# Three weight conversions behind the first layer norm, and other PSUM banks for two token products, in a fused scan, Fourier and MLP kernel

## The chip, the cores and the metric

The kernel runs on one core of one Trainium2 chip, as one launch. The metric is device microseconds from the first to the last moment of the execution, median over runs. The engines are named as the profile names them: PE (TensorE; PEld is its weight load), DVE (VectorE), ACT (ScalarE), POOL (GpSimd) and SP (the engine that issues all DMAs of this kernel).

## What is computed

All arrays are fp32: 4 batches, 8 heads, 768 tokens, head size 48, so 384 channels.

```python
# 1 a linear recurrence per head, complex decay a clipped to modulus 0.999
S = a[t] * S + outer(k[t], v[t]);  y[t] = q[t] @ Re(S)
# 2 Fourier mixing, then a layer norm and a channel MLP (384 -> 1536 -> 384)
u = x + Re(fft2(x));  un = layer_norm(u)
x = u + relu(un @ w_ch1) @ w_ch2
# 3 a token MLP (768 -> 256 -> 768), then a second channel MLP
u = x + (relu(x.T @ w_tok1) @ w_tok2).T
out = u + relu(u @ w_ch1b) @ w_ch2b
```

## The kernel before

Each batch goes through a **chain** and then through **dense** work. The chain is `stage1` (the scan over 48 steps and the attention-like sums per chunk of 96 tokens) and `stage2` (folds and mirrors of the transposed tokens, the real DFT as matmuls, the joins of its halves into six token tiles `u[0]` to `u[5]`, the layer norm into `un`). `stage2` handles its six tiles in three pairs (tile `i` and tile `i + 3`): a matmul result is copied out by ACT (L1188), POOL forms a difference and a sum of it (L1189, L1190), PE transposes the tokens (L1199), DVE joins both (L1204), and then come the statistics (L1211, L1212), a few tiny passes on ACT and DVE (L1221 to L1226), and one normalising pass for each tile, on DVE (L1233) or ACT (L1231). `LAST[0]` is the last normalising pass traced so far. `transposed` then turns `un` by PE and splits it in two fp32r halves, `th` (ACT, L1017) and `tl` (DVE, L1018).

Dense work is `dense1` (first channel MLP by `mlp`, then the token products `tok1` and `tok2`) and `mlp2` (second channel MLP). `mlp` runs in four quarters; each multiplies three weight blocks (L1034, with ReLU on ACT at L1038 and the low half on DVE at L1047) and adds the second product into `u` (L1056, L1059). Batch b's dense work fills PE while the chain of batch b + 1 runs; the buffer `qkt` exists once, so a scan follows the layer norm of the batch before. At the end the dense works of batches 2 and 3 are interleaved by `mixed`, and their `tok1` and `tok2` are called `late`.

**Conversions.** The weights arrive as 64-bit floats and are split into two fp32r halves on the chip. `convert` does one weight half of 128 x 384: a read into a tile of pool `T` (L206), ACT passes (L214 into a PSUM tile, L219), a DVE shift (L227), a POOL addition (L229), a DVE pass for the sign (L233), an ACT copy that rounds (L239), a POOL subtraction (L240) and a write to DRAM (`wscr`, L244). It is a generator: `tick` moves all generators in `active` on by one step, `feed` runs what is left to its end. Eight weights (p below 4) are kept in SBUF; twelve more (`back`) go through `convert` without a kept tile and are read again later (L320); the other 36 are converted during the first dense work by `lead`, in the form of L222 and L225, with the PSUM bank `c`, and the reads of the first few of these are ordered behind work of the MLP (`hold`).

Of the twelve, two are through before `stage2` of batch 0; **eight** are started at the sixth chunk and advanced once at the seventh (ACT passes); they are the eight in `active` when `stage2` reaches its five ticks (L1140, L1141). In order they hold the weights (13,0), (13,1), (14,0), (14,1), (15,0), (15,1), (4,1) and (6,1). The remaining two, (8,1) and (10,1), are done by `feed(56)` at L1321, after the first `transposed`.

**Order.** The program is traced in the order of the code; a planner then places every instruction on its engine's queue by priority and by a simulated time, and gives a tile its buffer when one of its pool is free. Priorities go by stream: for ACT, DVE and POOL the first chain and the dense work come first, then the conversions, then the other chains. `rests[0]` and `rests[1]` order a conversion's DVE passes and its POOL addition behind a given instruction in that plan (`rest`, `after`); this is an order of the planner, not a semaphore. Each engine then executes its queue in order, SP too.

**Buffers that matter.** Pool `T` has eight tiles: those of the conversions, and `th`, `tl`, `xh`, `xl`. PSUM has eight banks: two `s`, three `l`, two `p`, one `c`. A request for `s` takes turns over `s`, `s`, `c` (over `s` alone, or `s` and `p`, during the chain of batch 1). `p` holds the scans' state and the PSUM tile of the twelve conversions; `l` the MLPs' products. In the late calls `tok1` takes its two banks, and `tok2` and `transposed` theirs, from `s`.

Of the kernel before, what the change touches and what calls it, by code (L numbers as in the profile page):

```python
# [54 lines left out]
def attn_fft_mixer_kernel(ctx: ExitStack, tc: tile.TileContext, aL, xL, vL, wL, qN, kN, vN, arN, aiN,  # L55
# [37 lines left out]
    def alloc(tag, shape, dt=F32, name=None):  # L93
        n = 1
        for x in shape[1:]:
            n *= x
        t = pool.tile([128, SIZE[tag]], dt, tag=tag, bufs=BUFS[tag], name=name or tag)
        return shaped(t[0:shape[0], 0:n], shape)
# [4 lines left out]
    def palloc(tag, shape):  # L103
        n = 1
        for s in shape[1:]:
            n *= s
        if tag == "s":
            turn3[0] += 1
            tag = ("ssc", "s", "sp")[lent[0]]
            tag = tag[turn3[0] % len(tag)]  # L110
        t = psum.tile([128, 512], F32, tag=tag, bufs=PSB[tag], name=tag)
        v = t[0:shape[0], 0:n]
        if len(shape) == 3:
            v = v.rearrange("p (a b) -> p a b", b=shape[2])
        return v

    def r32(ap):
        return ap.bitcast(F32)
# [46 lines left out]
    LAST = [None]  # L165

    def marked(x):
        if stream[0] != CHAIN:
            mark[0] = x

    def after(x, y):
        tc.add_manual_dep(x.ins, y.ins.name, HOLD, reason="order of the streams")
# [6 lines left out]
    rests = [None, None]  # L179
# [72 lines left out]
    active, begun = [], []  # L252

    def begin():
        p, j = convs.pop(0)
        return convert(p, j, ws.place if (p, j) in early else None, far=True)

    def feed(n):

        keep, stream[0] = stream[0], BACK  # L260
        for _ in range(n):
            if convs:
                for _ in begin():
                    pass
        stream[0] = keep

    def tick(n, loads=False):

        keep, stream[0] = stream[0], BACK
        active[:] = [g for g in active if next(g, "end") != "end"]  # L270
        for _ in range(n):
            g = begin()
            next(g)
            if not loads:
                next(g)
            active.append(g)
        stream[0] = keep
# [790 lines left out]
    def stage2(b, space):  # L1068
# [50 lines left out]
        def dft(kt):  # L1119
            for ty in range(4):  # L1120
                n0, n = 128 * kt, ZK[ty][kt]
                ps = palloc("s", [128, 2, 97])
                for r in range(2):
                    for dt in range(2):
                        te.matmul(out=ps[0:n, r, :], lhsT=fd[:, ty, r, dt, n0:n0 + n], rhs=dcos[0:112, ty % 2, dt, r, :],
                                  start=(dt == 0), stop=(dt == 1))
                se.copy(out=Z[0:n, 2 * ty + kt, :].rearrange("p (i r) -> p r i", r=2), in_=ps[0:n])
# [7 lines left out]
        if b == 0:  # L1135
            for o, v in kept:
                after(sp.dma_start(out=o, in_=v), x)
            marked(x)
            rests[0], rests[1] = x, None
            for _ in range(5):  # L1140
                tick(0)  # L1141
            rests[0] = None
        dft(0)

# [94 lines left out]
    def tok1(b, u):  # L1239
        xh = [alloc("T", [128, 3, 384], F32R, name="xh") for _ in range(2)]  # L1240
        xl = [alloc("T", [128, 3, 384], F32R, name="xl") for _ in range(2)]
        xh, xl = ([x[i // 3][:, i % 3, :] for i in range(6)] for x in (xh, xl))
        for i in range(6):
            se.copy(out=xh[i], in_=u[i])  # L1244
            (ve if b in XL[0] and i in XL[1] else ge).tensor_tensor(out=xl[i], in0=u[i], in1=r32(xh[i]), op=ALU.subtract)  # L1245
        if EN:
            ws.ensure(b, 12, 0, 3)
        late = b in (B - 2, B - 1)
        if late:
            Rh, Rl = (alloc("tmp", [128, 2, 384], F32R, name="R") for _ in range(2))  # L1250
        else:
            R = alloc("h", [128, 4, 384], F32R, name="R")
            Rh, Rl = R[:, 0:2], R[:, 2:4]
        pss = [palloc("s" if late else "l", [128, 384]) for _ in range(2)]
        for part in (range(KS), range(KS, 6)):
            for m2, low in ((0, 0), (1, 0), (0, 1), (1, 1)) if part[-1] < 5 else ((0, 0), (0, 1), (1, 0), (1, 1)):
                for kt in part:
                    wh, wl = ws.block(b, 12 + m2, kt)
                    for w, x in (((wh, xl),) if low else ((wh, xh), (wl, xh))):
                        te.matmul(out=pss[m2], lhsT=w, rhs=x[kt], start=(kt == 0 and not low and w is wh),  # L1260
                                  stop=(kt == 5 and low == 1))
        if EN:
            ws.ensure(b, 14, 0, EN)
        for m2 in range(2):
            ps = pss[m2]
            se.activation(out=Rh[:, m2, :], in_=ps, func=ACTF.Relu)
            ve.scalar_tensor_tensor(out=Rl[:, m2, :], in0=ps, scalar=0.0, in1=r32(Rh[:, m2, :]),
                                    op0=ALU.max, op1=ALU.subtract)
        return Rh, Rl
# [13 lines left out]
    def dense1(b, u, th, tl):  # L1283
        go(mlp(u, b, 0, th, tl, None))
        R = tok1(b, u)
        g = tok2(b, u, *R)
        go(g, 2)
        return transposed(u, None, "l", g)
# [9 lines left out]
    def mixed(g, b, u):  # L1298

        go(g, 1)  # L1300
        R = tok1(b, u)
        go(g, 1)
        go(tok2(b, u, *R))
        go(g, 10)
        t = transposed(u, None, "s")
        go(g)
        return t


    def on(s, f, *args):  # L1310
        stream[0] = s
        return f(*args)

    def chain(b):
        return stage2(b, stage1(b))
# [2 lines left out]
    sp.dma_start(out=fk, in_=cFk)  # L1318
    u, norm = on(FIRST, chain, 0)
    t1 = on(FIRST, transposed, u, norm, "s")  # L1320
    feed(56)  # L1321
    for b in range(B - 2):
        lent[0] = int(not b)
# [21 lines left out]
    with tc.If(fv != 0):  # L1345
        with tc.For_i(0, B, 1) as b:
            fallback(b)
            u, norm = stage2(B, alloc("qk", [128, 12288], name="ws"))
            t = transposed(u, norm, "s")
            dense2(B, u, *dense1(B, u, *t), row=b)  # L1350
# [111 lines left out]
```

## Time and profile before

| | us |
|---|---|
| median of 3 runs | 1027.31 |
| lowest and highest of them | 1024.51, 1028.1 |
| the profiled execution | 1025.11 |
| its span, first to last instruction | 1023.2 |
| its mean granted TensorE clock | 0.991 of full |

The profile is of one execution. Its times are microseconds from the start of the span, unless marked ns. Matmuls are pipelined: a row of many has overlapping ends, so a busy PE is not PE at its peak. In a timeline, a row may stand for several like instructions (x2), and the bracket at its end gives the idle time of the engine before it and what ended it. "issue to landing" of a DMA is from the queue's instruction to the arrival of the last byte.

### The profile page before, as it was taken

To read this page: it belongs to the slowest core of one execution; us is meant where nothing else is said; L and a number is where in the kernel's file an instruction comes from. 1 tells how busy PE (TensorE), PEld (TensorE's weight loads), DVE (VectorE), ACT (ScalarE), POOL (GpSimd) and SP (SyncE) were. 2 spreads that over 40 slices of the span, in tenths; PEclk is the share of its full clock that TensorE was granted. 3 is DMA by queue.
4 is the path that set the end of the run, shared out by engine and by line. 5 is a ranking of instruction groups with operands and counts; after the bars stand their busy time and mean duration, and the time that the engine had idled before them with its cause. 6 is when DMAs were issued, how large, how long until landed. Compare 5 with 4: busy or idle time off the path is not lost.

```text
span 1023.2 us, 21015 instructions
## 1 busy us (share of the span) xinstructions
PE 951.0 (93%) x7312; PEld 902.0 (88%) x7312; DVE 716.9 (70%) x1965; ACT 526.4 (51%) x1489; POOL 452.8 (44%) x655
## 2 busy tenths in 40 slices
PE   1479989999899999999999999999999999999997
PEld 0338869999898899999998999999989999999997
DVE  7988978889897778999668889855664333433332
ACT  7864568887995166887216667821342122211111
POOL 7744677765785673677147335614630002000000
PEclk9999999999999999999999999999999999999999
DMA  6625865886689435665734467553325345435422
GB/s 234 175 67 140 290 269 165 283 268 210 212 258 272 146 95 187 193 179 174 206 110 140 129 193 247 157 149 102 108 78 166 131 131 171 139 108 176 136 91 80
DMA packets 98337, 173.09 MB, mean 169 GB/s; under 512 B 10928, under 2 KB 57904, under 8 KB 97712
## 3 DMA queue, kind: packets, MB, share of 16 engines
q1 hardware_dynamic: 98224, 171.67, 53.8%
q8 instruction: 60, 0.98, 0.4%
q14 instruction: 53, 0.43, 0.1%
HBM read 132.31 MB, written 39.32 MB: 168 GB/s over the span
## 4 chain that ended last, share of the span: by engine, by line
PE 66%; DVE 6%; ACT 3%; DMA 2%; POOL 2%; issue 2%; SPq 0%; POOLq 0%; ACTq 0%; DVEq 0%
PE l L1056 25%; PE l L1034 23%; DMA cvt<-wL 2%; PE s L845 2%; PE s L721 2%; PE l L1260 1%; PE l L1278 1%; PE s L1260 1%; PE s L1278 1%; PE s L1152 1%; DVE qkt L1099 1%; PE s L900 1%; PE s L860 1%; PE c L721 1%; PE c L845 1%
## 5 line engine op out<-in xcount | busy, mean ns | idle before, releaser
L1056 PE MATMUL l<-w,h 128*128 128x384 f32 x1728 | 324.0, 339 | 1.5 <-DVE h L1047 1.0
L1034 PE MATMUL l<-th,w 128*128 128x384 f32 x1152 | 313.3, 341 | 2.8 <-DVE h L1047 2.5
L1056 PEld LDWEIGHTS l<-w,h 128*128 128x128 f32 x1728 | 298.2, 188 | 3.5 <-DVE h L1047 2.0
L1034 PEld LDWEIGHTS l<-th,w 128*128 128x128 f32 x1152 | 209.1, 188 | 5.8 <-DVE h L1047 3.9
L1038 ACT ACTIVATE h<-l 128x384 fp32r<-128x384 f32 x192 | 94.0, 490 | 215.9 <-PE l L1034 215.3
L1034 PE MATMUL l<-tl,w 128*128 128x384 f32 x576 | 194.6, 338 | 0.0
L1059 DVE TENSOR_TENSOR u<-u,l 128x384 f32<-128x384 f32 x192 | 105.5, 549 | 74.4 <-PE l L1056 73.4
L1047 DVE SCALAR_TENSOR_TENSOR h<-l,h 128x384 fp32r<-128x384 f32 x160 | 88.3, 552 | 88.9 <-ACT h L1038 88.8
L1034 PEld LDWEIGHTS l<-tl,w 128*128 128x128 f32 x576 | 108.4, 188 | 0.1
L229 POOL TENSOR_TENSOR cvt<-cvt 128x384 int32<-128x384 int32 x48 | 50.4, 1051 | 27.4 <-DVE cvt L225 16.5
L1245 POOL TENSOR_TENSOR xl<-u,xh 128x384 fp32r<-128x384 f32 x18 | 18.0, 1014 | 93.2 <-ACT xh L1244 93.0
L240 POOL TENSOR_TENSOR w<-cvt,w 128x384 fp32r<-128x384 f32 x44 | 45.0, 1027 | 13.1 <-ACT w L239 13.0
L1045 POOL TENSOR_TENSOR h<-full,h 128x384 fp32r<-128x384 f32 x32 | 32.5, 1016 | 34.3 <-ACT full L1044 32.8
L529 PE MATMUL s<-misc,y 128*112 128x128 f32 x64 | 14.5, 369 | 35.4 <-DVE y L511 27.9
L694 DVE TENSOR_TENSOR p<-p,A 128x144 f32<-128x144 f32 x144 | 44.7, 310 | 2.8 <-ACT A L671 1.0
L529 PEld LDWEIGHTS s<-misc,y 128*112 128x112 f32 x64 | 9.3, 177 | 41.6 <-POOL ss L496 20.3
L881 POOL TENSOR_TENSOR yc<-Aa,gm 48x384 f32<-48x384 f32 x18 | 20.6, 1147 | 53.3 <-DVE Aa L871 53.0
L670 POOL TENSOR_TENSOR A<-raw,tm 128x144 f32<-128x144 f32 (+1 forms) x51 | 25.9, 508 | 39.4 <-DVE yt L695 29.6
L696 DVE TENSOR_TENSOR p<-p,yt 128x96 f32<-128x96 f32 x144 | 37.7, 262 | 2.8
L651 POOL TENSOR_TENSOR tm<-tm 128x144 f32<-128x144 f32 (+1 forms) x51 | 25.3, 496 | 32.3 <-ACT tm L650 27.8
L695 DVE TENSOR_TENSOR yt<-p,A 128x96 f32<-128x96 f32 x144 | 36.2, 251 | 2.4 <-ACT A L674 0.5
L721 PE MATMUL s<-misc,y 128*112 128x128 f32 x222 | 35.5, 273 | 1.2 <-DVE y L708 0.8
(320 smaller groups left out, 2045.2 us busy)
## 6 DMA issues: line engine op xcount, KB each, us to landing
w<-wscr SPq DMA_DIRECT2D x180, 384.0 KB, 3.5
cvt<-wL SPq DMA_DIRECT2D x48, 384.0 KB, 4.8
wscr<-w SPq DMA_DIRECT2D x44, 384.0 KB, 4.1
Kn<-kn SPq DMA_DIRECT2D x56, 192.0 KB, 3.7
kn<-y SPq DMA_DIRECT2D x96, 96.0 KB, 2.7
raw<-aL SPq DMA_DIRECT2D x48, 144.0 KB, 3.8
xx<-xL SPq DMA_DIRECT2D x48, 144.0 KB, 3.6
V<-vL SPq DMA_DIRECT2D x32, 144.0 KB, 3.0
```

The costliest lines, as they stand in the source:

```text
L229: x = ge.tensor_tensor(out=a, in0=a, in1=lo, op=ALU.add)
L240: ge.tensor_tensor(out=parts[:, 1, :], in0=a.bitcast(F32), in1=r32(parts[:, 0, :]), op=ALU.subtract)
L694: ve.tensor_tensor(out=cur, in0=prev, in1=A[:, j, 0:3, :], op=ALU.mult)
L695: ve.tensor_tensor(out=y, in0=prev[:, 1::-1, :], in1=A[:, j, 3:5, :], op=ALU.mult)
L696: ve.tensor_tensor(out=cur[:, 0:2, :], in0=cur[:, 0:2, :], in1=y, op=ALU.add)
L721: te.transpose(ps[:, j, :], y[:, j, 0:112], ident)
L1034: te.matmul(out=ps, lhsT=w1[:, wi, kt * 128:kt * 128 + 128], rhs=x[g][:, kt, :], start=(n == 0), stop=(n == 8))
L1038: x = se.activation(out=hi, in_=ps, func=ACTF.Relu)
L1045: ge.tensor_tensor(out=lo, in0=full, in1=r32(hi), op=ALU.subtract)
L1047: ve.scalar_tensor_tensor(out=lo, in0=ps, scalar=0.0, in1=r32(hi), op0=ALU.max, op1=ALU.subtract)
L1056: te.matmul(out=ps, lhsT=hs[m][:, hi, tt * 128:tt * 128 + 128], rhs=w2[:, wi, :], start=(n == 0), stop=(n == 8))
L1059: ve.tensor_tensor(out=u[tt], in0=u[tt], in1=ps, op=ALU.add)
```

## The change

In `stage2` of batch 0 the five ticks run over the first five of the eight conversions alone; the last three are set aside in `begun` and put back into `active` afterwards. In the main program, after the first layer norm and the first `transposed`, and ahead of `feed(56)`, five more ticks finish those three, with their DVE passes and POOL additions ordered behind `LAST[0]`, the last pass of that layer norm. Apart from that, `tok1` of batches 2 and 3 takes its two PSUM tiles from `p` and not from `s`.

```diff
--- before.py
+++ after.py
@@ -1137,8 +1137,10 @@
                 after(sp.dma_start(out=o, in_=v), x)
             marked(x)
             rests[0], rests[1] = x, None
+            active[:], begun[:] = active[:5], active[5:]
             for _ in range(5):
                 tick(0)
+            active[:], begun[:] = begun[:], []
             rests[0] = None
         dft(0)
 
@@ -1251,7 +1253,7 @@
         else:
             R = alloc("h", [128, 4, 384], F32R, name="R")
             Rh, Rl = R[:, 0:2], R[:, 2:4]
-        pss = [palloc("s" if late else "l", [128, 384]) for _ in range(2)]
+        pss = [palloc("p" if late else "l", [128, 384]) for _ in range(2)]
         for part in (range(KS), range(KS, 6)):
             for m2, low in ((0, 0), (1, 0), (0, 1), (1, 1)) if part[-1] < 5 else ((0, 0), (0, 1), (1, 0), (1, 1)):
                 for kt in part:
@@ -1318,6 +1320,10 @@
     sp.dma_start(out=fk, in_=cFk)
     u, norm = on(FIRST, chain, 0)
     t1 = on(FIRST, transposed, u, norm, "s")
+    rests[:] = [LAST[0]] * 2
+    for _ in range(5):
+        tick(0)
+    rests[:] = [None] * 2
     feed(56)
     for b in range(B - 2):
         lent[0] = int(not b)
```

## Rows read from the trace of the kernel before

**Rows 1.** The page: busy time of the engines; the chain that ended last, by line.
```profile
PE 951.0 (93%) x7312; PEld 902.0 (88%) x7312; DVE 716.9 (70%) x1965; ACT 526.4 (51%) x1489; POOL 452.8 (44%) x655
...
PE l L1056 25%; PE l L1034 23%; DMA cvt<-wL 2%; PE s L845 2%; PE s L721 2%; PE l L1260 1%; PE l L1278 1%; PE s L1260 1%; PE s L1278 1%; PE s L1152 1%; DVE qkt L1099 1%; PE s L900 1%; PE s L860 1%; PE c L721 1%; PE c L845 1%
```

**Rows 2.** Stages: length; busy us of PE, PEld, DVE, ACT, POOL; clock; DMA.
```profile
152.50:170.00 17.50, 17.50 (x93) 16.57 (x93) 13.08 (x31) 15.39 (x45) 11.30 (x18) 0.91 0.46 155
...
200.00:335.00 135.00, 127.50 (x955) 120.87 (x954) 115.58 (x322) 106.73 (x302) 91.67 (x128) 1.00 0.78 247
```

**Rows 3.** Groups by line, 125 to 152.5 us: count, busy us, mean ns, idle before.
```profile
L229 POOL TENSOR_TENSOR cvt<-cvt 128x384 int32<-128x384 int32 x8 | 8.1, 1019 | 7.3 <-DVE cvt L227 7.3
L240 POOL TENSOR_TENSOR cvt<-cvt 128x384 fp32r<-128x384 f32 x8 | 8.0, 1005 | 2.3 <-ACT cvt L239 2.3
...
L233 DVE SCALAR_TENSOR_TENSOR cvt<-p,cvt 128x384 int32<-128x384 int32 x8 | 4.4, 551 | 2.3 <-POOL cvt L229 2.1
L227 DVE TENSOR_SCALAR cvt<-p 128x384 int32<-128x384 int32 x8 | 4.3, 552 | 1.5 <-ACT p L214 1.5
...
L239 ACT CAST cvt<-cvt 128x384 fp32r<-128x384 f32 x8 | 4.0, 501 | 1.1 <-DVE cvt L233 1.1
```

**Rows 4.** Timeline of DVE: start, us, line, op, out<-in, count, idle before.
```profile
137.11 0.61 DVE L1204 TENSOR_TENSOR u<-c,qkt 128x192 f32<-128x192 f32 x2
...
145.71 0.55 DVE L233 SCALAR_TENSOR_TENSOR cvt<-p,cvt 128x384 int32<-128x384 int32 x1
146.17 0.61 DVE L1204 TENSOR_TENSOR u<-s,qkt 128x192 f32<-128x192 f32 x2
```

**Rows 5.** Line L1233: count, ns min/median/max, first and last start.
```profile
L1233 DVE TENSOR_SCALAR qkt<-u,mv,rs x3: 451/478/2264, 143.4 to 151.2; 128x384 f32<-128x384 f32 x3
```

**Rows 6.** Timeline of POOL.
```profile
141.59 1.00 POOL L240 TENSOR_TENSOR cvt<-cvt 128x384 fp32r<-128x384 f32 x1
...
143.53 0.53 POOL L1189 TENSOR_TENSOR qkt<-qkt 128x193 f32<-128x193 f32 x1
...
172.84 1.08 POOL L240 TENSOR_TENSOR w<-cvt,w 128x384 fp32r<-128x384 f32 x1
```

**Rows 7.** Timeline of ACT.
```profile
140.89 0.48 ACT L1188 COPY qkt<-s 128x386 f32<-128x386 f32 x1
...
151.76 0.72 ACT L1231 ACTIVATE qkt<-u,rs 128x384 f32<-128x384 f32 x1
...
164.53 0.20 ACT L684 COPY p<-A 64x48 f32<-64x48 f32 x1
```

**Rows 8.** Timeline of PE, at four places.
```profile
141.42 0.73 PE L1199 MATMUL s<-misc,xT 112*128 112x112 f32 x4 [0.57 <-ACT qkt L1188]
...
155.15 1.34 PE L1034 MATMUL l<-th,w 128*128 128x384 f32 x3
...
178.16 0.51 PE L1034 MATMUL l<-th,w 128*128 128x384 f32 x2
...
397.52 0.33 PE L1034 MATMUL l<-th,w 128*128 128x384 f32 x1
...
762.98 0.55 PE L1012 MATMUL c<-misc,qkt 128*128 128x128 f32 x3 [0.84 <-ACT qkt L1231]
```

**Rows 9.** Timeline of DVE at the second layer norm.
```profile
395.77 0.56 DVE L1018 TENSOR_TENSOR tl<-p,th 128x384 fp32r<-128x384 f32 x1 [0.30 <-ACT th L1017]
```

**Rows 10.** Timeline of SP's queue of DMA issues.
```profile
148.55 0.88 SPq L206 DMA_DIRECT2D cvt<-wL  x2
...
163.87 2.62 SPq L206 DMA_DIRECT2D cvt<-wL  x4
```

**Rows 11.** DMA issues: count, KB each, median us from issue to landing.
```profile
cvt<-wL SPq DMA_DIRECT2D x48, 384.0 KB, 4.8
...
wscr<-cvt SPq DMA_DIRECT2D x12, 384.0 KB, 3.7
```

**Rows 12.** Line L657, scan of batches 1 to 3: ns min/median/max.
```profile
L657 DVE SCALAR_TENSOR_TENSOR tm<-tm x51: 202/301/1160, 160.3 to 657.5; 128x144 f32<-128x144 f32 x48, 128x48 f32<-128x48 f32 x3
```

## The prediction

> **What bounds the kernel now.** I read the page first: TensorE (PE) is busy in 93% of the span, VectorE (DVE) in 70%, and 48% of the chain that ended last is the two matmul lines of the channel MLPs, L1034 and L1056 [rows 1]. The reader is to see there that from the first MLP to the end the kernel is one long queue of matmuls. So the time is: the start of that queue, its work, and its idle. The queue starts at 155.15 us [rows 8], after the first batch's scan, attention, Fourier stage and layer norm, which nothing overlaps. An edit before 155.15 can move the start; an edit after it pays only where PE sits idle.
>
> Next come the stages. From 200 to 335 us PE is busy for 127.5 of 135 us, but DVE also for 115.6, ScalarE (ACT) for 106.7 and GpSimd (POOL) for 91.7 [rows 2]: the scan of batch 1 and the conversions of 36 further weights run beside the first MLPs there. Just after the start, from 152.5 to 170 us, DVE has 13.1 busy of 17.5, ACT 15.4, POOL 11.3 [rows 2]. So there the room is 4.4, 2.1 and 6.2 us.
>
> Last come the instructions of the first layer norm, engine by engine [rows 4 to 7]. Eight conversions run through it. Each costs two DVE passes of 0.55 us, two POOL passes of 1.02 and 1.01, and an ACT pass of 0.50 [rows 3].
>
> **Part one, the layer norm.** The change takes the DVE and POOL passes of the last three of the eight out of it, and puts them behind its last pass, ACT's L1231 at 151.76 [rows 7]. The first five stay where they are. What goes is 6 x 0.55 = 3.3 us of DVE, 3 x 2.03 = 6.1 us of POOL, 3 x 0.50 us of ACT's L239 and, since only two PSUM banks feed the eight, also the last one's L214 on ACT (it needs the bank that the sixth frees; priced like L239, an estimate): 2.0 us. What decides is when the joins of the third pair of token tiles (L1204) start on DVE, now 146.17 [rows 4]. Three things must come first.
> - DVE itself. The first pair's joins end at 137.11 + 0.61 = 137.72, so 8.45 us lie between. In them are five passes of the moved conversions, 0.46 apart by the starts 145.71 and 146.17 [rows 4], together 2.3; and one normalising pass, L1233, of 2264 ns where the median is 478 [rows 5], 1.8 too long. Without them the joins could start at 146.17 - 4.1 = 142.1.
> - POOL's L1189. Its input, ACT's L1188, ends at 140.89 + 0.48 = 141.37 [rows 7]; it starts at 143.53, behind a subtraction at 141.59 and one more addition [rows 6], both of moved conversions. Without them it ends near 141.9.
> - PE's transposes L1199 end at 141.42 + 0.73 = 142.15 [rows 8]. They wait for L1188, which does not move.
>
> The three meet near 142.2, **4.0 us earlier**. From there to L1231 the same work follows, so the last pass comes at 147.8 and the first MLP at 151.2. Bounds: 2.2 if only POOL's wait goes (143.53 - 141.37); 5.6 if the lower clock goes too, since 0.91 of TensorE's clock was granted from 152.5 to 170 [rows 2], so part of it ran at 1.2 of 2.4 GHz, and 9% of 17.5 us is 1.6. I take 4.0; warm-up matmuls behind the last transposes stay as they are.
>
> **What part one pays back.** The moved work needs 3.3, 2.0 and 6.1 us on DVE, ACT and POOL where there is room for 4.4, 2.1 and 6.2: it just fits. If that cover were gone it would cost the next scan what ACT lacks, and ACT is the tightest: scan 1 cannot begin before its coefficients and its first product (L684, 164.53 [rows 7]). I let 2.0 us of ACT push it: scan 1 gains 2.0, not 4.0 (bounds 0 and 4.0). It matters where the two meet again, at the second layer norm. There the last split (L1018) ends at 395.77 + 0.56 = 396.33 [rows 9] and PE turns to the second batch's MLP at 397.52 [rows 8]: slack 1.2. So PE keeps 2.0 + 1.2 = **3.2** of its 4.0 us. The next stages repeat this with the next batch; I assume they pass 3.2 on.
>
> **The queues that the moved steps pass.** On SP the three writes (L244) go later. Behind them stand the reads (L206) of the two conversions that feed issues, then the next reads of scan data. One of those two reads now needs a buffer that a moved conversion frees only after the layer norm; its DMA chain is in the second rival. On DVE the held passes carry an order of the planner and no wait, so nothing stands behind them there longer than 0.55 us each. The transposes' four tiles of the same pool find their room among the first five conversions' buffers.
>
> **Part two, the token products.** It moves the first token product of batches 2 and 3 from the banks `s` to `p`, which the scans no longer use. Nothing is added or removed. Around it PE is idle 0.84 us before 762.98, where the last layer norm's transposes and this product both want `s` and `c` banks [rows 8]. With its own banks the product can fill such a hole. At most 0.84 is to be had; at worst the turns of `s` and `c`, which now fall on other tiles, lose as much. I take a gain of **0.4**.
>
> **Sum.** 3.2 + 0.4 = 3.6 us. The profiled execution took 1025.1 us, so it would take 1021.5; the median of the runs is 1027.3, 2.2 above it, and I put the forecast on the median: **1023.7**. With the bounds of these terms the gain is 0 + 1.2 - 0.8 = 0.4 at the low end and 5.6 + 0.8 = 6.4 at the high one, so 1020.9 to 1026.9. About 0.5% (5.1 us) is what a measurement of this kernel can tell from no change.
>
> **Rivals.**
> - *All of it arrives.* PE keeps the 4.0, the lower clock goes (1.6) and the idle 0.8 too: 6.4 us, **1020.9**. For it: PE idles little after 200 us, and batch 0 has matmuls left until 397.5. Against it: scan 1 must start as early as the MLP, beside more work. 0.25.
> - *The weights come late (slower).* The place is SP's queue. The last read of feed was issued with its neighbour in the pair at 148.55; 4.8 us to landing [rows 11] make it about 153.8, and SP reached the reads of the 36 weights at 163.87 [rows 10], 10.1 us on, just behind feed's writes. After the change this read waits for the sixth conversion: DVE, POOL, DVE, ACT, POOL from 147.8 make some 152, its write lands 3.7 later [rows 11], the read 4.8 after that, 160.5; with the same 10.1 SP gets to the weights at 170.6, 6.7 us late. The first of them is subtracted at 172.84 and ready at 173.9 [rows 6], and PE wants it at 178.3 [rows 8], 174.3 after the change. One stall only: 2.3 us slower than now, 1029.6. If the conversions pace the MLP from there, all 6.7 remain: **1034.0**. What decides is whether the planner lets the reads of the 36 overtake feed's last write on SP. For it: reads of weights are 2% of the chain [rows 1]. Against: the first weight now has 178.3 - 173.9 = 4.4 us of reserve. 0.13 for the whole stream.
> - *The moved passes lengthen scan 1.* L1233 took 2264 ns beside POOL passes and 451 at best [rows 5]; scan 1's L657 takes 301 ns in the median and up to 1160 [rows 12]. If half of the six POOL passes stretch such a pass by 0.86, DVE pays 2.6 + 3.3 against 4.0: 1.9 slower, **1029.2**. 0.10. The Trainium skill (GPSIMD Engine Reference, Specifications) says that POOL shares its SBUF interfaces with VectorE, so that both contend when VectorE runs in a two-port mode or reads two SBUF inputs, as L657 does; by that rule the move takes contention out of the layer norm and puts it into the scan, and both rows agree with it.
> - *It does not do what it says.* The planner orders all engines anew, the joins start by something else, and the gain ends below 1 us: **1027**. 0.10.
>
> **How the numbers follow.** The forecast has 0.42. Faster by over 0.5% (below 1022.2): the first rival and a ninth of the forecast's own range, 0.30. Slower by over 0.5% (above 1032.4): the late weights, 0.13. Within: 0.57. The range 1019.5 to 1031.0 leaves out the slow rival and the low end of the fast one.
>
> **What would show it.** Right: L1204's third group near 142, no L1233 over 0.6 us, the first L1034 near 151, L1018 of the second layer norm 2 us earlier, L1260 writing `p`. Wrong: a first L1034 after 153; a PE wait of over 2 us near 174 for a weight; idle of over 1 us before the second batch's MLP; SP standing at L244 beyond 165.

## The result, and the profile after

The changed kernel takes **1030.84 us** (median of 9 runs, 1028.70 to 1034.47) against 1025.61 for the kernel before on the same chip (9 runs, 1023.29 to 1028.20): ratio **1.0058**, 95% interval 1.0044 to 1.0072: 5.2 us slower by the medians, 5.9 by the ratio. The forecast was 1023.7, with 13% on slower by over 0.5%. All ratios below are to runs of the kernel before on the same chip, which took 1023.3 to 1025.6 us in the median; 0.001 is 1 us. In the changed kernel the lines above 1139 keep their numbers, those of the layer norm and the token products are two higher (L1204 is L1206).

The page of the changed kernel, part 1, against [rows 1]:

```profile
span 1030.6 us, 20995 instructions
PE 955.8 (93%) x7312; PEld 905.4 (88%) x7312; DVE 719.4 (70%) x1965; ACT 526.4 (51%) x1489; POOL 451.3 (44%) x655
```

The span is 7.4 us longer. TensorE's idle (span less busy) is 74.8 us for 72.2, so 2.6 of that is idle; the other 4.8 is busy time of the same 7312 matmuls. More busy time for the same work can come from the clock, although the mean granted clock, 0.990 for 0.991, makes only about 1 us of it over the whole span (an estimate: 1% of 1030.6 less 0.9% of 1023.2); where the rest comes from is not shown. So the first look goes to the clock in the stages of the layer norm (columns as in [rows 2]: length; busy us of PE, PEld, DVE, ACT, POOL; granted clock; DMA), the changed kernel first and one stage of the kernel before behind it:

```profile
125.00:132.50 7.50, 5.93 (x49) 5.62 (x47) 5.22 (x13) 5.33 (x14) 4.68 (x5) 0.99 1.00 363
132.50:139.50 7.00, 7.00 (x28) 6.91 (x28) 4.06 (x11) 3.27 (x8) 6.06 (x8) 0.53 0.94 378
139.50:146.00 6.50, 6.48 (x42) 5.09 (x41) 4.02 (x15) 2.52 (x10) 2.10 (x4) 1.00 0.44 149
```
```profile
132.50:139.50 7.00, 7.00 (x50) 6.74 (x48) 5.24 (x14) 3.97 (x9) 7.00 (x9) 1.00 0.90 363
```

POOL needs 12.85 us in these 21 us, for 17.50 before, as intended. But TensorE, fully busy from 132.5 to 139.5, was granted 0.53 of its clock: nearly all of that stretch ran at the lower of its two levels (1.2 of 2.4 GHz). The timeline of PE there, and of the ACT copy-outs (L1190, L1188 before) that follow from it:

```profile
131.51 1.36 PE L1125 MATMUL c<-dcos,qkt 112*128 112x97 f32 x8 [1.57 <-ACT qkt L1127]
132.67 2.83 PE L1154 MATMUL s<-qkt 128*128 128x193 f32 x8
...
136.79 3.94 PE L1154 MATMUL s<-qkt 128*128 128x193 f32 x16
```
```profile
140.77 0.48 ACT L1190 COPY qkt<-s 128x386 f32<-128x386 f32 x1 [3.04 <-PE s L1154]
143.86 0.48 ACT L1190 COPY qkt<-s 128x386 f32<-128x386 f32 x1 [1.95 <-PE s L1154]
...
150.37 0.71 ACT L1233 ACTIVATE qkt<-u,rs 128x384 f32<-128x384 f32 x1
```

In the kernel before, the two groups of 8 and 16 matmuls took 1.50 and 2.81 us:

```profile
132.68 1.50 PE L1152 MATMUL s<-qkt 128*128 128x193 f32 x8
...
134.95 2.81 PE L1152 MATMUL s<-qkt 128*128 128x193 f32 x16
```

The copy-out that stood at 140.89 [rows 7] comes at 143.86, the last normalising pass at 150.37 for 151.76 [rows 7], and the first MLP follows at 153.59 for 155.15 [rows 8]. The layer norm gained 1.4 us and not 4.0. The half clock was not new, though; it had changed its place. The kernel before had it at the layer norm's end, the changed kernel there had none (before first):

```profile
146.00:156.00 10.00, 7.26 (x25) 4.36 (x23) 7.74 (x26) 7.24 (x20) 3.23 (x5) 0.66 0.54 181
```
```profile
146.00:156.00 10.00, 8.38 (x38) 5.27 (x37) 9.03 (x27) 8.06 (x26) 4.55 (x7) 1.00 0.10 30
```

That alone would still be a gain. The loss arises later. In scan 1, at its twelfth step, ACT and DVE:

```profile
202.46 0.32 ACT L658 ACTIVATE tm<-tm 128x144 f32<-128x144 f32 x1 [0.77 <-DVE tm L657]
205.18 0.51 ACT L214 ACTIVATE c<-cvt 128x384 f32<-128x384 f32 x1 [2.40 <-DMA cvt<-wL]
205.63 0.53 ACT L219 ACTIVATE cvt<-cvt 128x384 int32<-128x384 uint32 x1
206.06 0.53 ACT L222 ACTIVATE cvt<-cvt 128x384 fp32r<-128x384 int8 x1
...
207.31 0.33 ACT L671 COPY A<-A 128x144 f32<-128x144 f32 x1
```
```profile
206.62 0.56 DVE L225 SCALAR_TENSOR_TENSOR cvt<-c,cvt 128x384 int32<-128x384 int32 x1 [2.65 <-ACT cvt L222]
207.67 0.32 DVE L694 TENSOR_TENSOR p<-p,A 128x144 f32<-128x144 f32 x1 [0.49 <-ACT A L671]
```

Read it from below. The scan's step (L694) waits for ACT's L671; L671 stands in ACT's queue behind the passes of a conversion (L214 to L222); L214 waits 2.40 us for that conversion's read. L671's own input, from POOL's L670, was there by 204.3 at the latest. ACT executes its queue in order, so the scan stands behind a transfer that it has nothing to do with. In the kernel before there is the same wait for the same kind of read, but the scan's pass had gone ahead of it:

```profile
199.91 0.32 ACT L671 COPY A<-A 128x144 f32<-128x144 f32 x1
...
204.00 0.51 ACT L214 ACTIVATE c<-cvt 128x384 f32<-128x384 f32 x1 [2.21 <-DMA cvt<-wL]
```

From there on the chains are late. The table gives the starts of steps 12 and 14 of scan 1 (step 14 shows how much of the lateness stays) and of the last normalising pass of each batch, in us, from the timelines of DVE and ACT; three kernels of the experiments stand beside. Each column is one profiled execution.

| | before | changed | hold undone, order of the changed kernel kept | changed, one place repaired | hold alone, order of before |
|---|---|---|---|---|---|
| batch 0, last pass | 151.8 | 150.4 | 152.4 | 149.6 | 147.6 |
| scan 1, step 12 | 200.3 | 207.7 | 208.8 | 202.8 | 198.6 |
| scan 1, step 14 | 206.1 | 210.8 | 212.0 | 208.1 | 204.0 |
| batch 1, last pass | 390.8 | 397.5 | 402.3 | 391.7 | 387.0 |
| batch 2, last pass | 583.4 | 594.7 | 600.2 | 586.4 | 579.6 |
| batch 3, last pass | 762.2 | 773.9 | 779.5 | 765.6 | 758.4 |

TensorE itself also loses time further on, in the chain of batch 2. In the changed kernel it waits there 2.95 us, its longest wait behind the first MLP's start, for a read of `Kn` (what the scan wrote, read back for the sums per chunk); matmuls of the token product stand behind it in the queue, and part of what follows runs at half clock. In the kernel before the same group of matmuls starts without a wait. First these matmuls, then the stretch from 500 to 510 us, the changed kernel first each time:

```profile
504.01 0.23 PE L860 MATMUL s<-V,Kn 96*64 96x48 f32 x1 [2.95 <-DMA Kn<-kn]
```
```profile
494.95 0.26 PE L860 MATMUL s<-V,Kn 96*64 96x48 f32 x1
```
```profile
500.00:510.00 10.00, 7.05 (x71) 6.62 (x71) 5.75 (x14) 0.96 (x2) 0.00 (x0) 0.83 0.69 171
```
```profile
500.00:510.00 10.00, 10.00 (x151) 9.05 (x151) 6.11 (x13) 2.01 (x4) 3.34 (x4) 1.00 0.56 157
```

Whether the late chain alone makes this second wait, or the order of TensorE's own queue too, no run separates.

### The profile page after: what moved, and what is told of

Same layout as the page of the kernel before. It is cut to its first block, busy times and chain, and to the rows that moved or that the text cites. A ratio compares the mean times of both kernels' runs of the same rounds, so it can differ in the third digit from the quotient of the medians.

```text
span 1030.6 us, 20995 instructions
## 1 busy us (share of the span) xinstructions
PE 955.8 (93%) x7312; PEld 905.4 (88%) x7312; DVE 719.4 (70%) x1965; ACT 526.4 (51%) x1489; POOL 451.3 (44%) x655
## 4 chain that ended last, share of the span: by engine, by line
PE 47%; DVE 2%; DMA 2%; POOL 1%; ACT 0%; issue 0%; SPq 0%; POOLq 0%
PE l L1056 18%; PE l L1034 18%; PE s L845 2%; PE p L1262 1%; PE s L1280 1%; PE s L900 1%; PE s L721 1%; DMA kn<-y 1%; PE c L845 1%; PE s L906 1%; PE s L860 1%; PE s L1154 1%; PE c L900 0%; PE s L1012 0%; DMA V<-vL 0%; DMA Kn<-kn 0%
## 5 line engine op out<-in xcount | busy, mean ns | idle before, releaser
L1034 PE MATMUL l<-th,w 128*128 128x384 f32 x1152 | 313.6, 342 | 3.8 <-DVE h L1047 3.2
L1034 PEld LDWEIGHTS l<-th,w 128*128 128x128 f32 x1152 | 209.2, 189 | 6.5 <-DVE h L1047 4.2
L1034 PE MATMUL l<-tl,w 128*128 128x384 f32 x576 | 194.4, 338 | 0.0
L1059 DVE TENSOR_TENSOR u<-u,l 128x384 f32<-128x384 f32 x192 | 105.2, 549 | 75.5 <-PE l L1056 74.8
L1034 PEld LDWEIGHTS l<-tl,w 128*128 128x128 f32 x576 | 108.5, 188 | 0.7 <-DVE tl L1018 0.6
L694 DVE TENSOR_TENSOR p<-p,A 128x144 f32<-128x144 f32 x144 | 44.8, 311 | 3.4 <-ACT A L671 1.2
L696 DVE TENSOR_TENSOR p<-p,yt 128x96 f32<-128x96 f32 x144 | 37.7, 262 | 2.8
L670 POOL TENSOR_TENSOR A<-raw,tm 128x144 f32<-128x144 f32 (+1 forms) x51 | 25.9, 508 | 26.1 <-DVE tm L668 13.6
```

What stands on the lines that cost most here:

```text
L694: ve.tensor_tensor(out=cur, in0=prev, in1=A[:, j, 0:3, :], op=ALU.mult)
L696: ve.tensor_tensor(out=cur[:, 0:2, :], in0=cur[:, 0:2, :], in1=y, op=ALU.add)
L1034: te.matmul(out=ps, lhsT=w1[:, wi, kt * 128:kt * 128 + 128], rhs=x[g][:, kt, :], start=(n == 0), stop=(n == 8))
L1059: ve.tensor_tensor(out=u[tt], in0=u[tt], in1=ps, op=ALU.add)
```

## The experiments

The theories, by the letters that the expectations use. **A**: the moved passes cost scan 1 more than the layer norm gains (A1: their DVE time does). **B**: the banks of part two make the loss (B2, B3: the later writes and reads on SP's queue do). **C**: half clock in the Fourier product takes the gain (C2: in part of the executions). **D**: the planner's new order of everything makes it, whatever the edit was (D1: one place of that order, D2: many). **E**: TensorE's slack takes an earlier layer norm away.

**First, the parts, a dose, and the clock.** The two parts alone; the hold for one conversion only; and the change with fillers for TensorE's wait before 131.51.

```diff
-            active[:], begun[:] = active[:5], active[5:]
+            active[:], begun[:] = active[:7], active[7:]
```

> Part one alone (three conversions held, tok1 keeps its s banks). Theory A (the hold reorders the plan of scan 1 and the chains of batches 1 and 2 arrive 7 and 11 us late; part two is worth nothing): +4 to +8 us, and the last norm pass of layer norm 2 between +4 and +8 us later than in before. Theory B (the loss comes from the s/p banks of part two): within 1 us of before. Theory C (TensorE fell to half clock by chance of the order): part one alone has again a stretch of half clock between 125 and 146 us, and +3 us or more; without that stretch it gains 2 to 3 us on before.

> Part two alone. Theory A and C: within 1.5 us of before (the part two stretch of the changed kernel is less than 1 us different). Theory B: +4 us or more, with the lag arising after 700 us.

> As the changed kernel, but only the eighth conversion (6,1) is held behind the layer norm. If the loss is a dose effect of the moved DVE and POOL passes on scan 1 (theory A as a price per conversion): a third of +5.2 us, +1 to +2.5 us on before. If it is set by which order the plan happens to take (theory D: every edit reorders all that follows, and the time scatters by some us whatever the dose): anything between -4 and +8 us, out of line with the dose.

```diff
+                if b == 0 and kt == 0 and ty == 3:
+                    warm(4, wide)
                 ps = palloc("s", [128, 2, 97])
```

> The changed kernel with four more filler matmuls (128x512) in the 1.6 us in which TensorE waits ahead of the last type of the Fourier product. Theory C (half clock ate the layer norm's gain): granted clock 1.00 from 125 to 146 us, the second copy-out of ACT 2.5 to 3 us earlier, the last norm pass at 147.5 to 148.5 us and not 150.4, and the end 2 to 4 us earlier than the changed kernel if what follows hands the gain on. Theory A: layer norm earlier, but the end within 1.5 us of the changed kernel, as scan 1 is set by the conversions. Theory D: the end moves out of proportion, by over 4 us either way.

Measured: the hold alone 1.0067 (1.0040 to 1.0095); part two alone **0.9982** (0.9971 to 0.9993); one conversion held 1.0108 (1.0086 to 1.0130); the change with fillers 1.0057 (1.0037 to 1.0077). B falls: part two gains 1.8 us, and where is seen below. A as a price per conversion falls: a third of the dose costs 11 us, more than the whole. In its profiled execution the run with fillers had a clock of 1.00 from 125 to 146 us, but the fillers shifted the last pass to 151.23, and it ended no faster (D, too, had expected the end to move, by over 4 us): C alone does not explain the loss. The hold alone says it more plainly: in its profiled execution TensorE had full clock from 125 to 146 us and the last pass came at 146.59, 5.2 us earlier than before, and yet that execution ended 5.5 us later (span 1028.7 for 1023.2).

**Then, edits that should be free.** The three conversions' passes from the DVE shift on left out, in the place of before and in the held place; and two numbers of filler matmuls in the kernel before, one of them a single further one.

```diff
+        if (p, j) in ((15, 1), (4, 1), (6, 1)):
+            yield
+            sp.dma_start(out=wscr[p][j], in_=t[:, 0:2 * n].bitcast(F32).rearrange("p (k n) -> p k n", k=2))
+            return
...
-                warm(4, wide, tp)
+                warm(5, wide, tp)
```

> The kernel before, with the DVE, POOL and ACT passes after the third step of the three conversions (15,1), (4,1), (6,1) left out (their reads, their two ACT passes and their writes stay, in the place of before; what they write to DRAM is not the split weight). Nothing is moved into scan 1, so this prices what the layer norm's gain is worth at the end. Theory A (the loss is what the moved passes cost in scan 1): layer norm 2 to 4 us earlier and the end 3 to 4 us earlier than before. Theory E (PE's slack takes an earlier layer norm away): layer norm earlier, end within 1 us of before. Theory D (the order of the plan decides): the end moves by over 4 us either way.

> The changed kernel with the same passes left out of the three held conversions, so that the hold moves only their writes. Theory A: the moved passes are the cost, so the end comes within 1.5 us of the run above (1019 to 1022 us). Theory B2 (the hold itself, by the later writes and reads on SP's queue, makes the loss): 1028 to 1031 us still. Theory D: out of line with both.

> The kernel before with the same four filler matmuls ahead of the last type of the Fourier product. Before showed no half clock between 125 and 146 us, so theory C gives at most 0.5 us either way. Theory D: any change of the order moves the end, by 3 us or more.

> The kernel before with one more filler matmul at the end of the joins (five for four), a change that costs nothing by itself. Theories A and C: within 1 us of before. Theory D: 3 us or more from before, and then 5 us of the changed kernel can't be told from the plan's scatter.

Measured: 1.0078 (1.0065 to 1.0091) with work taken out of the kernel before; 1.0037 (1.0023 to 1.0050) with it taken out of the changed one; **1.0149** (1.0129 to 1.0170) for four fillers, **1.0189** (1.0164 to 1.0213) for one. A single matmul of half a microsecond costs 19.5 us. Only D expected such a thing: every edit lets the planner order all engines anew, and none of the eight kernels so far that got a new order, the changed one included, met the time of before. Part two alone is the exception that fits: in its trace the order stayed nearly that of before (15 of 1965 DVE instructions moved). A comparison of two kernels under a free plan then says little about the edit.

**So the order had to be held.** In the following kernels the wrapper through which all instructions are issued gives each of them its place in the order of before as its priority, and ties it behind its predecessor there on the same engine (an order of the planner, no semaphore). What the edit touches (the three conversions, and the two of `feed`) finds its place anew; of SP's transfers only the conversions' are tied (in the filler's run all). Tied instructions share the wrapper's line in the profile.

```diff
-            tc.cur_priority = RANK[self.kind][stream[0]] * 100000 + count[0]
+            tc.cur_priority = at[0]
...
+                    tc.add_manual_dep(x.ins, row[i - 1][1].ins.name, HOLD, reason="order")
```

> The kernel before with one more filler matmul at the end of the joins, but every other instruction tied to its place in the order of before on its engine. The same filler with a free plan cost 19.5 us. Theory D (the order of the plan makes the time): within 1 us of before. If the filler itself cost the 19.5 us (the clock, or TensorE's time): +10 us or more again.

> The hold alone (part one, with tok1 in its s banks), every other instruction of PE, DVE, ACT and POOL tied to the order of before; only the three held conversions, the two that feed does and SP's other transfers find their places anew. Theory D: the loss of 6.9 us of the hold with a free plan is gone, and the gain that the layer norm leaves shows: last norm pass 2 to 4 us earlier, end between 0 and 4 us earlier than before (my on-record sum for this part: 3.2 us earlier). Theory A (the moved passes themselves cost scan 1 more than the layer norm gains): +3 to +7 us also with the order held. Theory E (slack takes the gain): within 1 us of before.

> The whole change, order of all else held as in the run above. Theory D: the run above less the 1.3 to 1.8 us that part two gave alone: 2 to 5 us earlier than before, and 7 us or more earlier than the changed kernel. Theory A: +1 to +5 us.

> The kernel before, order of all else held, with the passes of the three conversions from the DVE shift on left out (their writes carry what the buffer holds, not the split weight). With a free plan this cost 7.6 us. It prices a layer norm without those passes and with nothing put into scan 1. Theory D: 2 to 4 us earlier than before; the difference between this and the hold with the order held is what the passes cost behind the layer norm: under 1 us if scan 1 has room for them, 3 us if DVE (3.2 us of passes) sets scan 1's pace.

Measured: the filler 0.9996 (0.9977 to 1.0015), for 1.0189 before: the filler costs nothing, its new order cost 19.5 us. The hold **1.0007** (0.9986 to 1.0028), for 1.0067; the whole change 1.0013 (0.9991 to 1.0034), for 1.0058; the passes left out 0.9974 (0.9956 to 0.9991), for 1.0078. So E falls as a whole answer: without the moved passes 2.7 us of an earlier layer norm do reach the end. D is right on the loss, but its other half missed: it expected the hold 0 to 4 and the whole change 2 to 5 us faster than before. In its profiled execution the hold did in the layer norm what the forecast said, and the end came 4.2 us earlier than in the profiled execution of before:

```profile
span 1019.0 us, 21013 instructions
```
```profile
147.59 0.72 ACT L433 ACTIVATE qkt<-u,rs 128x384 f32<-128x384 f32 x1
```

But that was its fastest run: the twelve spread from 1020.9 to 1029.0, with a median of 1026.3 (the kernel before on that chip: 1021.1 to 1029.7 in 35 runs, median 1024.3), and the change with the order held, profiled at 1028.6, had its last pass at 152.09. So without the new order the hold is worth nothing that can be measured here, in the median.

**The reverse, and one place.** The hold undone while the order of the changed kernel is kept (part two stays in); the changed kernel in its own order but for four instructions (the conversion's L214, L219, L222 and L225 behind step 12's L671, L674, L694 to L696); and, for the hold's lost gain, the late writes without the passes. The second, as the order of the two queues by line:

```diff
-ACT: L658 L214 L219 L222 L239 L731 L732 L671 L1038 L674
+ACT: L658 L239 L731 L732 L671 L1038 L674 L214 L219 L222
-DVE: L225 L694 L1047 L695 L696
+DVE: L694 L1047 L695 L696 L225
```

> The reverse of the held order: the hold undone (the three conversions pass through the layer norm as in before; tok1 in its p banks), but every other instruction of PE, DVE, ACT and POOL tied to the order of the changed kernel. Theory D (the order that the plan took makes the loss): +3 to +8 us on before although nothing is held. If the hold itself made the loss: within 1.5 us of before less the 1.8 us of part two, so -3 to 0 us.

> The changed kernel, its order held, but for four instructions: the three ACT passes and the DVE pass of the conversion whose late read held up step 12 of scan 1 (2.4 us of ACT's wait, 2.65 of DVE's) stand behind that step's scaling passes and state update and not ahead of them. Theory D1 (that one place makes the lag of the chains): step 12 comes 3 to 4 us earlier, at 204 and not 207.7 us, the last norm pass of layer norm 1 still 2 us or more earlier, and the end 2 to 4 us earlier. Theory D2 (the loss is spread over many places of the order): step 12 earlier, the end within 1.5 us of the changed kernel.

> The hold with the order of before held, the passes of the three conversions left out, and their writes ordered behind the layer norm as the hold has them. Between the layer norm without those passes (-2.7 us) and the hold with them (+0.7 us) lie 3.4 us. Theory A1 (the passes take that time on DVE behind the layer norm): this run at -2 to -3.5 us. Theory B3 (the late writes keep the buffers and delay the two last reads and what follows on SP's queue): this run at -0.5 to +1.5 us.

Measured: **1.0080** (1.0060 to 1.0100) with nothing held. ACT waits at the same place:

```profile
206.35 0.51 ACT L432 ACTIVATE c<-cvt 128x384 f32<-128x384 f32 x1 [2.60 <-DMA cvt<-wL]
...
208.47 0.32 ACT L432 COPY A<-A 128x144 f32<-128x144 f32 x1
```

The order makes the loss, then, and the hold is not needed for it; nor does tying the order cure it by itself. The one place repaired gives **1.0012** (0.9990 to 1.0034), 4.6 us less than the changed kernel's 1.0058 (interval of the difference 2.0 to 7.2, from the two). By the traces the four instructions are all that moved: behind 115 us no other instruction of ACT, DVE, POOL or SP changed its place. The wait for the read is still there, shorter, and the scan's two passes now stand ahead of it:

```profile
202.44 0.32 ACT L425 COPY A<-A 128x144 f32<-128x144 f32 x1
202.65 0.50 ACT L425 ACTIVATE h<-l 128x384 fp32r<-128x384 f32 x1
203.03 0.33 ACT L425 ACTIVATE A<-A 128x144 f32<-128x144 f32 x1
204.07 0.52 ACT L425 ACTIVATE c<-cvt 128x384 f32<-128x384 f32 x1 [0.71 <-DMA cvt<-wL]
```

Step 12 starts at 202.8 for 207.7, and the table shows 5.8 of the 6.7 us of batch 1's lateness gone (0.8 of them from an earlier layer norm in that execution). D1 holds in the medians: four of the 3454 instructions of ACT and DVE make most of the loss. The second place, TensorE's wait for `Kn`, is still there, shorter:

```profile
497.27 1.10 PE L425 MATMUL s<-V,Kn 96*64 96x48 f32 x32 [2.15 <-DMA Kn<-kn]
```

So the order has more than one bad place.

The late writes without the passes gave 0.9988 (0.9971 to 1.0006), between the two that they were to tell apart, and within the interval of either: what takes back the layer norm's gain, the 3.3 us of DVE passes or the late writes, is not settled.

**Last, the clock once more.** In the changed order-held kernel the profiled execution (152.09) had TensorE at half clock where the hold's (147.59) had full clock; changed kernel with the order of before first, the hold alone second:

```profile
132.00:138.50 6.50, 6.27 (x25) 6.18 (x26) 2.59 (x5) 3.05 (x8) 5.37 (x8) 0.50 1.03 414
```
```profile
132.50:139.50 7.00, 7.00 (x48) 6.25 (x47) 4.74 (x15) 3.43 (x10) 6.24 (x9) 1.00 1.03 413
```

The fillers of the run above, now with the order held, on the change, on the kernel before, and on part two alone:

> The whole change with the order of before held, and four filler matmuls (128x512) in TensorE's wait of 1.6 us ahead of the last type of the Fourier product. With the order held, one execution without half clock in the Fourier product had the last norm pass at 147.6 and ended 3.8 us earlier than before; one with 6.8 us of half clock there had it at 152.1 and ended 3.6 us later. Theory C2 (the clock in the Fourier product takes the hold's gain away in part of the executions): granted clock 1.00 from 125 to 146 us, last norm pass at 147 to 149 us, median 3 to 6 us below before (1018 to 1021 us), and a spread narrower than the 9 us of the run without filler. If the clock there is not what splits the executions: within 1.5 us of before and as wide a spread.

> Control: the kernel before, order held, with the same four fillers. With a free plan these cost 15.6 us. Theory C2 and D: within 1.5 us of before, as before showed no half clock there in its profiled execution; a gain of 1 to 2 us if some executions of before have it too. If the fillers by themselves are worth more (TensorE busy for another 1.9 us): 2 us or more either way.

> The control with part two added and no hold. Against the whole change with fillers this prices the hold itself, on one chip and with one order. If the hold is worth its layer norm's gain less what the moved passes cost: the whole change is 2 to 4 us faster than this. If the hold is worth nothing: both within 1.5 us of each other, 1 to 3 us below before.

Measured: 1.0027 (1.0013 to 1.0041), 1.0009 (0.9992 to 1.0026), 1.0007 (0.9991 to 1.0024). C2 falls as an answer. In the profiled execution of the change the clock was 1.00 and TensorE busy throughout, but the median is no lower. The spread was 5.4 us, which is no sign either: the kernel before spread 5.6 us on that chip.

```profile
125.00:146.00 21.00, 21.00 (x124) 16.58 (x123) 13.72 (x43) 11.63 (x32) 12.84 (x16) 1.00 0.83 308
```

The fillers delay the last type of the Fourier product (133.24 us, for 130.72 in the hold's profile), and the last normalising pass comes at 150.01: 1.8 us earlier than before, yet the end is later. With the order held and the fillers in, the hold comes out 2.0 us slower (1.0027 against 1.0007), but the interval of the difference, -0.2 to 4.2, does not exclude nothing; part two is worth nothing that this pair can show (1.0007 against 1.0009, interval of the difference -2.6 to 2.2, which has room for the 1.8 us). No version here beats both kernels clearly but part two alone, at 0.9982 in its one comparison.

## Why the prediction was wrong

**The step that failed** stands in what part one pays back: "scan 1 gains 2.0, not 4.0", and behind it the sum's tacit assumption that all instructions that the change does not move keep their order. They did not. Instead of coming 2.0 us earlier, scan 1 was 7.4 us late at its twelfth step and 4.7 at its fourteenth. By the longest common order of the two traces, at least 339 of the 1965 DVE instructions and 355 of the 1489 of ACT stand elsewhere in their queues than before; with the order held it is 23 and 16. The new order cost 4.5 us (1.0058 against 1.0013, interval of the difference 1.9 to 7.1), and I had it in a rival ("the planner orders all engines anew", at 0.10) that could cost no more than the gain. Five edits under a free plan (one conversion held, passes left out twice, fillers twice) lost 4 to 19.5 us, where the like edits with the order held moved the time by -2.7 to +0.9: that is the size it should have had.

**The layer norm's term** (4.0 us) was right as a mechanism. With the order held the last pass came at 147.59, forecast 147.8, and the first MLP at 151.38, forecast 151.2. The 2264 ns pass is gone in the changed kernel too:

```profile
L1235 DVE TENSOR_SCALAR qkt<-u,mv,rs x3: 467/477/479, 144.2 to 149.8; 128x384 f32<-128x384 f32 x3
```

The profiles of the other runs bear out what stretched that pass. In the six executions in which it took 1.3 us or more (1312, 1716, 1722, 2261, 2264 and 2270 ns), a row of POOL passes without a gap ran beside it and it ended 0.22 us behind the last of them; where POOL was idle it took 435 to 481 ns. It is not stretched each time, though: in the run with five fillers it took 485 ns beside POOL passes.

In the changed kernel only 1.4 came, with TensorE's matmuls at half clock ahead of it. My bounds of 2.2 to 5.6 let the half clock at the layer norm's end go, which it did, and let none come elsewhere.

**The room in scan 1** was right in kind and under-priced: the moved work was to fit but for 2.0 us, and with the order held about all that the layer norm gains is lost later. Without the passes 2.7 us remain at the end (0.9974); with them nothing does (1.0007). I had let 2.0 us of ACT push scan 1; the 3.3 us of DVE may be the price, but that is not shown, as the run that was to decide between them and the late writes did not.

**The slow rival on SP's queue** showed its sign and not its harm. SP issued feed's last write at 170.86, about where the forecast had it reach the 36 weights (170.6), but the reads of these had overtaken it from 164.20 on:

```profile
164.20 0.33 SPq L206 DMA_DIRECT2D cvt<-wL  x1
164.88 0.32 SPq L244 DMA_DIRECT2D wscr<-cvt  x1
165.30 0.38 SPq L206 DMA_DIRECT2D cvt<-wL  x1
...
170.86 0.33 SPq L244 DMA_DIRECT2D wscr<-cvt  x1
```

PE shows no wait from 170 to 180 us. The read that ACT waits for at step 12 of scan 1 came 1.2 us later than in the kernel before (L214 starts at 205.18 for 204.00), a small part of that step's 7.4; whether the hold made it late is not shown. **The rival of stretched passes** has no support: scan 1's L657 takes 208, 301 and 1143 ns (least, median, most), for 202, 301 and 1160 [rows 12]. Of the rule that went with it, the interfaces that POOL shares with VectorE (the Trainium skill, GPSIMD Engine Reference, Specifications), the layer norm shows the one half, its long pass beside POOL's gone; no run shows contention put into the scan.

**Part two** (0.4, at most 0.84) was under-sized. Alone it gained 1.8 us (0.7 to 2.9). The hole it fills is not the one before 762.98 only: with the order of before otherwise kept, the product starts between the last layer norm's transposes, while those still wait, and PE is idle nowhere from 760 to 800 us, for 1.3 us in the kernel before (part two alone):

```profile
757.77 2.59 PE L1260 MATMUL p<-xh,w 128*128 128x384 f32 x14
760.20 0.49 PE L1012 MATMUL s<-misc,qkt 128*128 128x128 f32 x3
```
```profile
760.00:800.00 40.00, 40.00 (x241) 39.81 (x240) 17.22 (x32) 9.66 (x22) 1.49 (x2) 1.00 0.51 165
```

That profiled execution ended 4.7 us earlier than that of before (span 1018.5), but 3.2 of these it had already ahead of the moved products (a group of L1034 starts at 722.37 for 725.53); the group behind them starts at 791.20 for 796.17, so 1.8 us arise here.

In the changed kernel the last layer norm is 11.7 us late, and the product comes behind four of its six transposes; PE waits 0.79 us there, now for the product's own input:

```profile
769.90 2.38 PE L1262 MATMUL p<-xh,w 128*128 128x384 f32 x12 [0.79 <-ACT xh L1246]
```

**What stays open**: why executions of one kernel differ by 8 us on that chip, those of the kernel before (1021.1 to 1029.7) as well as those of the hold with the order held (1020.9 to 1029.0). Half clock in the Fourier product does not sort them: the execution of the whole change with the order held had it and took 1028.6 us, but the repaired kernel's had it too (0.50 from 131 to 137.5 us) and took 1023.8, and the one with the fillers took 1029.8 without it.

## What to carry to other kernels

Where a planner orders the queues, an edit has two effects, what it does and what order it brings; before you size the first, measure the second with an edit that does nothing, and hold the order when you compare. In an order, look for work that waits for a transfer and stands ahead of a step of the critical chain on an in-order engine: moving four such instructions was worth 4.6 us here, and moving three conversions nothing that could be measured. A gain in one stage that moves its work into a stage where that engine is nearly full may be no gain: here nothing of it was left in the median.

## What the runs showed that I had not expected

One filler matmul cost 19.5 us by the order it brought and nothing (0.9996) with the order held. And the same wait of TensorE, 1.57 us for ACT's L1127 ahead of the last type of the Fourier product, was followed by half clock in the changed kernel and by full clock in the hold with the order of before, so that wait alone does not decide it. The latter, on PE:

```profile
130.72 1.13 PE L433 MATMUL c<-dcos,qkt 112*128 112x97 f32 x8 [1.57 <-ACT qkt L433]
```

What TensorE did ahead of it was not quite the same. An earlier wait, ahead of the Fourier product's first matmuls, was 1.50 us in the changed kernel and 0.86 in the hold:

```profile
120.62 1.08 PE L1125 MATMUL s<-dcos,qkt 112*65 112x97 f32 x8 [1.50 <-DVE qkt L1109]
```
```profile
119.82 1.08 PE L433 MATMUL s<-dcos,qkt 112*65 112x97 f32 x8 [0.86 <-DVE qkt L433]
```

Whether that decides, no run here tells.
